# Adaptive-LN attention block on one core: the rounding of the weights' pieces from ScalarE to GpSimd, one transpose half a cycle later, and three portions of work moved behind empty ones

## The chip, the core and the metric

The kernel runs on one core of a Trainium2 chip. The metric is the device time of one execution in microseconds (us). A profiled execution also has a span, from its first to its last instruction; its own time is a little longer than that.

## What is computed

The input x is 2048 tokens by 512 features, in float32. Six rows of 512 come from silu(c) times a weight matrix; they scale, shift and gate the two halves of a transformer block:

```python
h = _layernorm(x, axis=-1) * (1 + ca) + sa
x = x + ga * _A_ref(h, A_wq, A_wk, A_wv, A_wo)
h = _layernorm(x, axis=-1) * (1 + cb) + sb
x = x + gb * _B_ref(h, B_w1, B_w2)
```

_A_ref is attention with 32 query heads of width 16 that share one key and one value head; scores are scaled, softmaxed over all 2048 keys, multiplied into the values and projected by wo. _B_ref is two dense layers, 512 to 1792 to 512, with a ReLU between them.

## The kernel before, in words

**Precision.** Many matmuls take their operands as float32r, a rounded float32. To keep accuracy, an operand is split in two pieces: a high piece, which is the value rounded to float32r, and a low piece, the rest. The product then takes three matmuls (high by high, high by low, low by high; `thrice`, L470). The helper `split` (L239) makes the pieces: ScalarE rounds with a Copy activation (L240) and GpSimd subtracts (L241). It serves weights, queries, the attention's output (`oh`, `ol`), the second layer norm's output (`hh`, `hl`), the hidden layer (`r4`) and the row maxima (`ms`).

**The main loop.** Attention is done in 32 units: 8 blocks of 256 tokens by 4 groups of 8 heads. A unit has 16 key tiles of 128. The loop at L884 runs 256 cycles, two key tiles each, so a unit lasts 8 cycles. A cycle has two parts, and the order of TensorE's work in each is written out by hand in `PARTS` (L40), one letter per step:

```python
PARTS = "cbcuaucuaucuau", "bldlbldlbldlad"
```

"c" and "d" are score matmuls, each into one of three PSUM banks `ps_exp`, which ScalarE reads with an Exp (L768, L770). "a" and "b" are the score matmuls of a later unit, into three banks `ps_max`, whose row maxima VectorE takes (L426, L428). "u" and "l" are the upper and lower 64 rows of a portion of other matmuls, the filling, all into the single bank `ps_fill` (L163). Each part ends with `values` (L872, L878), eight recorded matmuls into `ps_pv`; in the timeline one such group stands at the end of each part. The stretch between two such groups is called a half below, and cycles are counted from c = 0.

**Where other work hangs.** `advance` (L864) is the last piece of the sixth "l", that is near the end of part 2 of a cycle: it asks the generator of the filling for the next portion, and whatever the generator does between two portions is put into the engines' queues there. Work in the list `put_off` is issued in the next cycle's first part, after its fourth step (L913). Work in `half_later` is issued in the second part, after its second step (L916). At the end of a cycle the steps in `ends` that are due are issued (L920), and then one step of `chores` (L923). Each engine, and SP, which issues the DMAs, takes its instructions strictly in the order in which they were issued.

**Chores.** In c = 0 to 34 `chores` (L719) prepares the weights, one generator begun per cycle: 14 column blocks of w1 (`first_layer`: load, split, store the pieces to DRAM `w1dr`), 4 row blocks of wo (`projection`: load, multiply by the gate on GpSimd, split into `woh` and `wol`) and 14 row blocks of w2 (`second_layer`, the same into `w2r`). From c = 2 to 33 one split falls at the end of each cycle. The raw blocks rotate through three buffers.

**Filling.** In c = 0 to 32 the filling is the projection of queries 3 to 13 (`others_of`, L708), three portions each, of float32 matmuls; after the third, `end` (L341) copies the bank to `stg` on ScalarE (L248) and puts off the split into `qq` and the three stores to DRAM (`to_dram`, L337). From c = 33 on, each block b = 0 to 6 has 32 cycles of filling by `behind(b)` (L511), one portion per cycle: three portions `rest`, four of the output projection, seven of `fill`, fourteen of the first dense layer, four of the second. For b > 0, `fill` is the second dense layer of the block before. For the first of them, b = 0, `rest` is query 14, and `fill` is query 15 (three portions) and four empty ones (L527); an empty portion is replaced by six matmuls whose result nobody reads (L898). The two `qq` tiles of b = 0 share three buffers `w1s` with the tiles that first-layer weights are loaded into (`load_w1`, L450).

**The second layer norm.** While `fill` runs, `second_norm` (L557) goes one step further at each `advance`. Its steps: put off `norm_of(0)`, which normalises the first tile of 128 tokens (a few small VectorE and GpSimd instructions, then three large ones on GpSimd); statistics of the second tile on VectorE; `norm_of(1)` and `turn_of(0)`; `turn_of(1)` by way of `half_later`; two cycles on, four loads of `xh` from DRAM `xdr`; and put off the split of `xh` into `hh` and `hl`, which the first dense layer needs in the cycle after. `turn_of` (L542) transposes a tile in 32 by 32 blocks on VectorE (`xt`, L544) and stores it to `xdr` (L546, on SP's queue). In this kernel block b = 0 does these steps in c = 39 to 45; block b = 1 does them 32 cycles later, and so on.

**The end of a unit.** `normalise` (L773) copies `ps_pv` to `pvs` on ScalarE (L780) at the end of a unit's last cycle, c = 7, 15, 23 and so on. Two cycles later `back` (L803) takes reciprocals (L804) and issues `recs` (L805) and `den` (L806) on SP; `den` must wait for `recs` to land.

The last block is finished by `behind_last` after the loop; it doesn't touch the changed lines.

Of the kernel before, what the change touches and what calls it, by code (L numbers as in the profile page):

```python
# [9 lines left out]
F32 = mybir.dt.float32  # L10
# [3 lines left out]
OP = mybir.AluOpType  # L14
# [42 lines left out]
def build(tc, nc, cst, sb, ps, dr, x, wq, wk, wv, wo, w1, w2, c, w_mod, out):  # L57
# [8 lines left out]
    def ps_fill():  # L66
        return ps.tile([P, 512], F32, name="ps_fill", tag="fill", bufs=1)
# [51 lines left out]
    woh = cst.tile([P, DC, D], F32R, name="woh")  # L119
    wol = cst.tile([P, DC, D], F32R, name="wol")  # L120
# [118 lines left out]
    def split(hi, lo, src, eng=None):  # L239
        nc.scalar.activation(hi, src, AF.Copy)  # L240
        (eng or nc.gpsimd).tensor_tensor(lo, src, hi.bitcast(F32), op=OP.subtract)  # L241

    def stage():
        return sb.tile([P, 512], F32, name="stg", tag="stg", bufs=3)
# [11 lines left out]
    put_off, half_later = [], []  # L256

    def add_psum(dst, pt, other):
        stg = stage()
        nc.scalar.activation(stg, pt, AF.Copy)  # L260
        nc.gpsimd.tensor_tensor(dst, stg, other, op=OP.add)  # L261
# [185 lines left out]
    w2r = []  # L447
# [13 lines left out]
    def flat(t, k2):  # L461
        return t[:, k2 * 2:k2 * 2 + 2].rearrange("p a n -> p (a n)")

    def open_block(b):
        x1 = sb.tile([P, TT, D], F32, name="x1", tag="x1", bufs=2)
        nc.sync.dma_start(x1, chunks(x[b * TB:(b + 1) * TB]))
        x1s[b] = x1
        return x1, [sb.tile([P, DC, TB], F32R, name=n, tag="t4", bufs=2) for n in ("oh", "ol")]
# [23 lines left out]
    def dense2(b, t, pt):  # L492
        ts = slice(t * P, (t + 1) * P)
        todo = []
        for f in range(FC):
            i, fi = divmod(f, 8)
            rh, rl = r4s[b][i * 2], r4s[b][i * 2 + 1]
            w = w2r[f // 2]
            for n, (a, p) in enumerate(((rh, 0), (rh, 1), (rl, 0))):
                todo.append(("f32r", pt, a[:, fi, ts], w[:, p, f % 2],  # L500
                             f + n == 0, f == FC - 1 and n == 2))
        return todo
# [8 lines left out]
    def behind(b):  # L511
        def in_parts(todo, n):
            for i in range(0, len(todo), n):
                yield todo[i:i + n]

        def second(b, t):
            pt = ps_fill()
            yield from in_parts(dense2(b, t, pt), 6)
            ot = sb.tile([P, D], F32, name="ot", tag="tmp", bufs=2)
            add_psum(ot, pt, x1s[b][:, t])  # L520
            nc.sync.dma_start(out[b * TB + t * P:b * TB + (t + 1) * P], ot)

        x1, oo = open_block(b)
        if b == 0:
            qqs = [sb.tile([P, 2, LB], F32R, name="qq", tag="w1s", bufs=3) for _ in range(2)]
            rest, fill = [others_of(14 + n, qqs[n]) for n in range(2)]
            fill = itertools.chain(fill, [[]] * 4)  # L527
        else:
            rest, fill = carried.pop(), second(b - 1, 1)
        yield next(rest)  # L530
        yield next(rest)
        for k2 in range(DC // 2):
            put_off.append(partial(split, flat(oo[0], k2), flat(oo[1], k2), flat(on[b], k2)))
        yield from rest
        xn = sb.tile([P, TT, D], F32, name="xn", tag="xn", bufs=1)
        xdr = dr.tile([32, TT, 4, D], F32, name="xdr", tag="xdr", bufs=2)
        mvs = [ln_mv(1) for t in range(TT)]

        def norm_of(t):
            normed(x1, xn, (t,), *ln_stats(mvs[t], 1, False), nc.gpsimd)  # L540

        def turn_of(t):  # L542
            xt = sb.tile([P, D], F32, name="xt", tag="tmp", bufs=2)
            nc.vector.transpose(xt.rearrange("p (j k n) -> p k j n", j=4, k=DC),  # L544
                                xn[:, t].rearrange("p (k j n) -> p k j n", j=4, k=DC))
            nc.sync.dma_start(xdr[:, t].rearrange("a i n -> i a n"), xt)  # L546

        for t in range(TT):
            pt = ps_fill()
            for n, part in enumerate(in_parts(out_proj(pt, oo, t), 6)):  # L550
                yield part
                if t and n == 0:
                    ln_sums(mvs[0], 0, x1[:, 0])
            add_psum(x1[:, t], pt, x1[:, t])
        ahead = [load_w1(f) for f in range(2)]

        def second_norm():  # L557
            put_off.append(partial(norm_of, 0))
            yield
            ln_sums(mvs[1], 0, x1[:, 1])  # L560
            yield
            norm_of(1)
            turn_of(0)
            yield
            half_later.append(partial(turn_of, 1))
            yield
            yield
            xh = sb.tile([P, TT * 4, DC, 32], F32, name="xh", tag="xn", bufs=1)
            pieces = xdr.rearrange("a t i (j m) -> j a (t i) m", j=4)
            for j in range(4):  # L570
                nc.sync.dma_start(xh[j * 32:(j + 1) * 32].rearrange("p q k n -> p q (k n)"),
                                  pieces[j])
            yield
            for k2 in range(DC // 2):
                ks = slice(k2 * 2, k2 * 2 + 2)
                put_off.append(partial(split, *[h[:, ks].rearrange("p k (q n) -> p k q n", n=32)
                                                for h in hp],
                                       xh.rearrange("p q k n -> p k q n")[:, ks]))
            yield

        norm2 = second_norm()
        next(norm2)
        hp = [sb.tile([P, DC, TB], F32R, name=n, tag="t4", bufs=2) for n in ("hh", "hl")]
        for n, part in enumerate(fill):
            yield part
            next(norm2, None)
        r4 = r4s[b] = [sb.tile([P, 8, TB], F32R, name="r4", tag="big", bufs=4) for _ in range(4)]
        for f2 in range(FC // 2):
            pt = ps_fill()
            for f in range(f2 * 2, f2 * 2 + 2):  # L590
                if f + 2 < FC:
                    ahead.append(load_w1(f + 2))
                yield dense1(pt[:, (f % 2) * TB:(f % 2 + 1) * TB], ahead.pop(0), hp)
            i, f = divmod(f2 * 2, 8)
            put_off.append(split_psum(
                r4[i * 2][:, f:f + 2].rearrange("p a n -> p (a n)"),
                r4[i * 2 + 1][:, f:f + 2].rearrange("p a n -> p (a n)"), pt, AF.Relu))
        first_half = second(b, 0)
        yield from itertools.islice(first_half, 4)
        carried.append(first_half)  # L600
# [118 lines left out]
    def chores():  # L719


        def first_layer(f):
            raw = sb.tile([P, DC, P], F32, name="raw", tag="stg", bufs=3)
            nc.sync.dma_start(raw, chunks(w1[:, f * P:(f + 1) * P]))
            yield
            yield
            parts = sb.tile([P, 2, DC, P], F32R, name="w1s", tag="w1s", bufs=3)
            split(parts[:, 0], parts[:, 1], raw)
            yield
            nc.sync.dma_start(w1dr[f].bitcast(F32), parts.bitcast(F32))  # L730
            yield

        def projection(i):
            raw = sb.tile([P, D], F32, name="raw", tag="stg", bufs=3)
            nc.sync.dma_start(raw, wo[i * P:(i + 1) * P])
            yield
            nc.gpsimd.tensor_tensor(raw, raw, gr[:, 0], op=OP.mult)
            yield
            split(woh[:, i], wol[:, i], raw)
            yield  # L740
            yield

        def second_layer(f):
            raw = sb.tile([P, D], F32, name="raw", tag="stg", bufs=3)
            nc.sync.dma_start(raw, w2[f * P:(f + 1) * P])
            yield
            nc.gpsimd.tensor_tensor(raw, raw, gr[:, 1], op=OP.mult)
            yield
            if f % 2 == 0:
                w2r.append(sb.tile([P, 2, 2, D], F32R, name="w2r", tag="wt", bufs=7))  # L750
            split(w2r[-1][:, 0, f % 2], w2r[-1][:, 1, f % 2], raw)
            yield
            yield

        todo = [first_layer(f) for f in range(FC)] + [projection(i) for i in range(DC)] \
            + [second_layer(f) for f in range(FC)]
        for n in range(len(todo) + 3):

            for g in todo[max(0, n - 3):n + 1]:
                next(g)  # L760
            yield
# [122 lines left out]
    for c in range(NU * KT // 2):  # L884
# [5 lines left out]
        if places:  # L890
            u, i, j = places.pop(0)
# [69 lines left out]
```

## Time and profile before

| | us |
|---|---|
| three executions: median | 1662.97 |
| lowest and highest of the three | 1656.94, 1666.34 |
| the profiled execution's own time | 1652.57 |
| its span | 1650.8 |
| PE, DVE, ACT, POOL busy in the span | 1631.9, 1359.6, 1220.1, 361.7 |

PE is TensorE's matmuls, PEld its weight loads, DVE is VectorE, ACT ScalarE, POOL GpSimd, and SPq the queue of SyncE, which issues DMAs. A row of the view of stretches gives a stretch of the span from A to B, its length, and the busy time of each engine in it with the number of instructions. A row of the timeline gives a start, a busy time, the engine, the line, the operation, what it writes and reads, and in brackets how long the engine was idle just before and whose end let it go on. Durations of instructions on one engine overlap a little, since the next one enters before the last one has drained.

### The profile page before, as it was taken

Reading aid. Unit: us, or ns where it says so; the run is one execution under the profiler, and the core shown is the slowest. Engines: PE = TensorE matmul, PEld = TensorE weight load, DVE = VectorE, ACT = ScalarE, POOL = GpSimd, SP = SyncE. Lnnn points to the kernel's source line nnn. Section 1 sums busy time; section 2 is a strip of 40 time slices with the busy share of each in tenths; the row PEclk is TensorE's granted clock in tenths of the full one; section 3 lists DMA queues with packets and bytes.
Section 4 is the critical chain, followed back from the end, with each engine's and each line's share of the span. In section 5 each row is a group of like instructions: output and inputs, shape, how many; then the busy total and the mean of one; then the engine's idle time right before and its main releaser. Section 6 shows DMA issues by size and latency. Waiting matters only on the chain.

```text
span 1650.8 us, 33967 instructions
## 1 busy us (share of the span) xinstructions
PE 1631.9 (99%) x13018; PEld 918.2 (56%) x13018; DVE 1359.6 (82%) x2371; ACT 1220.1 (74%) x2385; POOL 361.7 (22%) x524
## 2 busy tenths in 40 slices
PE   8999999999999999999999999999999999999999
PEld 5445555555655565546654565446654565556568
DVE  7888888898889988898889888898889888897031
ACT  4248888877877788778877787778877888778831
POOL 3103355331103211131103211131113211131110
PEclk9999999999999999999999999999999999999999
DMA  8115543223301231113301231113211231113331
GB/s 287 51 51 161 186 128 111 88 71 99 104 17 49 73 105 55 43 56 105 93 28 38 74 117 43 62 42 110 83 30 39 84 106 41 61 43 102 122 113 57
DMA packets 97544, 137.19 MB, mean 83 GB/s; under 512 B 25644, under 2 KB 60396, under 8 KB 97384
## 3 DMA queue, kind: packets, MB, share of 16 engines
q1 hardware_dynamic: 95672, 134.90, 26.5%
q8 instruction: 104, 1.70, 0.4%
q14 instruction: 56, 0.46, 0.1%
q10 hardware_dynamic: 1712, 0.13, 0.1%
HBM read 104.00 MB, written 28.82 MB: 80 GB/s over the span
## 4 chain that ended last, share of the span: by engine, by line
PE 90%; ACT 4%; DVE 2%; DMA 1%; issue 1%; SPq 0%; POOL 0%; POOLq 0%; ACTq 0%; DVEq 0%
PE ps_pv L878 29%; PE ps_exp L768 21%; PE ps_max L426 18%; PE ps_fill L163 16%; ACT pe L770 3%; PE ps_exp L146 2%; PE ps_max L146 1%; DVE pm L428 1%; PE ps_fill L146 1%; PE ps_exp L307 1%; PE ps_exp L190 1%; DMA wmod<-in_w_mod_dram 0%; DMA xdr<-xt 0%; PE ps_exp L293 0%; PE ps_fill L190 0%
## 5 line engine op out<-in xcount | busy, mean ns | idle before, releaser
L428 DVE TENSOR_REDUCE pm<-ps_max 128x1 f32<-128x512 f32 x2048 | 1272.5, 682 | 166.2 <-PE ps_max L426 140.9
L770 ACT ACTIVATE pe<-ps_exp 128x512 f32<-128x512 f32 x2048 | 1080.7, 606 | 290.7 <-PE ps_fill L163 134.3
L426 PE MATMUL ps_max<-kp,qp 48*128 48x512 f32 x2048 | 846.4, 426 | 1.1 <-DVE pm L428 0.3
L768 PE MATMUL ps_exp<-qp,kp 50*128 50x512 f32 x2048 | 763.4, 414 | 5.0 <-ACT pe L770 3.3
L878 PE MATMUL ps_pv<-pe,vt 128*32 128x512 f32 x4096 | 545.5, 605 | 0.0
L426 PEld LDWEIGHTS ps_max<-kp,qp 48*128 48x128 f32 x2048 | 372.5, 185 | 274.6 <-DVE pm L428 240.4
L768 PEld LDWEIGHTS ps_exp<-qp,kp 50*128 50x128 f32 x2048 | 360.2, 185 | 267.0 <-ACT pe L770 180.2
L163 PE MATMUL ps_fill<-w2r,r 64*128 64x512 f32 x1044 | 288.8, 405 | 0.0
L163 PE MATMUL ps_fill<-hh,w1s 64*128 64x256 f32 x1568 | 229.0, 285 | 0.0
L163 PEld LDWEIGHTS ps_fill<-hh,w1s 64*128 64x128 f32 x1568 | 204.5, 186 | 6.7 <-PEq L156 6.7
L163 PEld LDWEIGHTS ps_fill<-w2r,r 64*128 64x128 f32 x1044 | 181.9, 185 | 7.1 <-PEq L156 2.5
L878 PEld LDWEIGHTS ps_pv<-pe,vt 128*32 128x32 f32 x4096 | 80.5, 108 | 125.9 <-issue 105.7
L241 POOL TENSOR_TENSOR r<-stg,r 128x512 fp32r<-128x512 f32 x49 | 62.7, 1280 | 320.6 <-ACT r L240 303.7
L163 PE MATMUL ps_fill<-hl,w1s 64*128 64x256 f32 x784 | 126.8, 281 | 0.0
L163 PE MATMUL ps_fill<-hT,wq 64*128 64x256 f32 x416 | 118.2, 399 | 0.0
L163 PEld LDWEIGHTS ps_fill<-hl,w1s 64*128 64x128 f32 x784 | 105.8, 186 | 0.0
L922 POOL TENSOR_TENSOR on<-num,den 128x256 f32<-128x256 f32 x31 | 22.8, 737 | 244.9 <-DMA den<-recs 204.9
L163 PEld LDWEIGHTS ps_fill<-hT,wq 64*128 64x128 f32 x416 | 70.2, 185 | 2.9
L784 POOL COPY num<-pvs 128x256 f32<-128x256 f32 x32 | 12.7, 397 | 173.5 <-ACT pvs L780 173.5
L261 POOL TENSOR_TENSOR x<-stg,x 128x512 f32<-128x512 f32 x14 | 18.2, 1297 | 97.9 <-ACT stg L260 97.9
L633 DVE TENSOR_TENSOR ol<-on,oh 128x256 fp32r<-128x256 f32 (+1 forms) x3 | 2.1, 714 | 44.2 <-ACT oh L629 44.2
L248 ACT ACTIVATE stg<-ps_fill 128x512 f32<-128x512 f32 x62 | 38.3, 617 | 0.0
(145 smaller groups left out, 931.0 us busy)
## 6 DMA issues: line engine op xcount, KB each, us to landing
w1s<-w1dr SPq DMA_DIRECT2D x104, 512.0 KB
qdr<-qq SPq DMA_DIRECT2D x48, 256.0 KB
qp<-qdr SPq DMA_DIRECT2D x128, 96.0 KB
raw<-in_B_w_dram SPq DMA_DIRECT2D x28, 256.0 KB
w1dr<-w1s SPq DMA_DIRECT2D x14, 512.0 KB
wmod<-in_w_mod_dram SPq DMA_DIRECT2D x6, 1024.0 KB
x<-in_A_x_dram SPq DMA_DIRECT2D x8, 512.0 KB
out_dram<-ot SPq DMA_DIRECT2D x16, 256.0 KB
```

The costliest lines, as they stand in the source:

```text
L146: nc.tensor.matmul(pt, w, a, start=start, stop=stop)
L163: ins = nc.tensor.matmul(pt, w[r], a[r], start=start and h == 1, stop=stop and h == 0)
L190: nc.tensor.matmul(pt, sgw[:, k], wm[i][:, k], start=k == 0, stop=k == DC - 1)
L241: (eng or nc.gpsimd).tensor_tensor(lo, src, hi.bitcast(F32), op=OP.subtract)
L248: nc.scalar.activation(stg, pt, func, **kw)
L261: nc.gpsimd.tensor_tensor(dst, stg, other, op=OP.add)
L426: nc.tensor.matmul(pt, qps[u][i][r, j * P:(j + 1) * P], kp[r, kb * 512:(kb + 1) * 512], start=True, stop=True)
L428: nc.vector.tensor_reduce(pms[u][:, (i * 2 + hf) * 4 + j, kb:kb + 1], pt, axis=AX.X, op=OP.max)
L768: nc.tensor.matmul(pt, kp[r, kt * P:(kt + 1) * P], qps[u][ct // 2][r], start=True, stop=True)
L770: nc.scalar.activation(pe, pt, AF.Exp)
L878: nc.tensor.matmul(pvt[i * 32:(i + 1) * 32], vt[:, kt], pes.pop((s, i)), start=(kt == 0), stop=(kt == KT - 1))
L922: due[1]()
```

## The change

- In the three chores `split` is replaced by a new helper, `split_pool`, which has GpSimd do the rounding as well as the subtraction. That is 14 + 4 + 14 = 32 roundings of a 128 x 512 block; all other splits stay.
- `turn_of(0)` isn't issued at `advance`, straight behind `norm_of(1)`, but put off: it comes in the first part of the next cycle, after its fourth step. It does so in all seven blocks.
- For b = 0, `fill` is three empty portions, the three of query 15 and one empty portion, in place of the three of query 15 and four empty ones.

```diff
+    def split_pool(hi, lo, src):
+        nc.gpsimd.tensor_copy(hi, src)
+        nc.gpsimd.tensor_tensor(lo, src, hi.bitcast(F32), op=OP.subtract)
...
-            fill = itertools.chain(fill, [[]] * 4)
+            fill = itertools.chain([[]] * 3, fill, [[]])
...
             norm_of(1)
-            turn_of(0)
+            put_off.append(partial(turn_of, 0))
             yield
             half_later.append(partial(turn_of, 1))
...
-            split(parts[:, 0], parts[:, 1], raw)
+            split_pool(parts[:, 0], parts[:, 1], raw)
...
-            split(woh[:, i], wol[:, i], raw)
+            split_pool(woh[:, i], wol[:, i], raw)
...
-            split(w2r[-1][:, 0, f % 2], w2r[-1][:, 1, f % 2], raw)
+            split_pool(w2r[-1][:, 0, f % 2], w2r[-1][:, 1, f % 2], raw)
```

## The prediction

> **What bounds the kernel now.** I read the page first, then lengths of stretches, then single halves. The page's span, engines and chain:
>
> ```profile
> span 1650.8 us, 33967 instructions
> PE 1631.9 (99%) x13018; PEld 918.2 (56%) x13018; DVE 1359.6 (82%) x2371; ACT 1220.1 (74%) x2385; POOL 361.7 (22%) x524
> PE 90%; ACT 4%; DVE 2%; DMA 1%; issue 1%; SPq 0%; POOL 0%; POOLq 0%; ACTq 0%; DVEq 0%
> ```
>
> TensorE is the bound; GpSimd is on the chain nowhere. The change takes no matmul away, so all that it can win is places where TensorE waits. They show in the lengths of stretches, cut where `ps_pv` groups start (view of stretches: length, then PE, PEld, DVE, ACT, POOL busy):
>
> ```profile
> 106.55:118.11 11.56, 11.56 (x89) 6.29 (x87) 9.84 (x17) 8.36 (x17) 0.00 (x0) 1.00 0.55 155
> 106.55:313.63 207.08, 204.29 (x1496) 107.56 (x1494) 176.09 (x293) 173.18 (x343) 82.88 (x73) 1.00 0.46 139
> 402.72:482.77 80.05, 80.05 (x744) 47.87 (x742) 70.48 (x119) 65.02 (x129) 10.38 (x12) 1.00 0.23 69
> 280.82:284.01 3.19, 3.08 (x24) 1.37 (x23) 2.81 (x5) 3.19 (x8) 1.12 (x1) 1.00 0.04 8
> 316.46:319.31 2.85, 2.85 (x23) 1.34 (x22) 2.46 (x5) 2.80 (x7) 0.04 (x1) 1.00 0.00 0
> 197.85:201.30 3.45, 3.08 (x24) 1.37 (x23) 3.06 (x5) 3.30 (x8) 1.51 (x2) 1.00 0.52 191
> 388.32:391.30 2.98, 2.98 (x30) 1.88 (x28) 2.58 (x5) 2.78 (x7) 0.40 (x1) 1.00 0.57 176
> 537.55:540.94 3.39, 3.32 (x24) 1.33 (x23) 3.32 (x9) 2.85 (x7) 1.64 (x9) 1.00 0.07 8
> 546.63:549.46 2.83, 2.83 (x24) 1.55 (x22) 2.51 (x6) 1.82 (x5) 0.70 (x1) 1.00 0.62 185
> 351.56:355.17 3.61, 3.52 (x22) 1.45 (x21) 3.54 (x10) 3.07 (x7) 1.79 (x10) 1.00 0.07 10
> 377.94:382.62 4.68, 3.36 (x24) 1.42 (x22) 3.13 (x7) 3.08 (x7) 2.38 (x2) 1.00 0.17 46
> ```
>
> The third row is 14 quiet cycles, 5.72 us each, so a half is about 2.85 and there TensorE is never idle. The first is c = 0 and 1, before any weight is split: 5.78 a cycle, since float32 query portions cost a little more. The second is all 35 cycles of the chores. At 5.78 they would take 202.3; they take 207.1. **So the chores' stage holds 4.8 us of waiting, and no more can be won there.** The other rows are single halves: the undisturbed kind is 2.85, the rest are what the change goes for.
>
> **Part 1: rounding on GpSimd.** The half from 280.82 takes 3.19 us with ScalarE busy all through. Its ScalarE timeline, and the weight load that waited:
>
> ```profile
> 281.20 0.62 ACT L248 ACTIVATE stg<-ps_fill 128x512 f32<-128x512 f32 x1
> 281.67 0.63 ACT L770 ACTIVATE pe<-ps_exp 128x512 f32<-128x512 f32 x1
> 282.15 0.66 ACT L240 ACTIVATE w2r<-raw 128x512 fp32r<-128x512 f32 x1
> 282.67 1.12 ACT L770 ACTIVATE pe<-ps_exp 128x512 f32<-128x512 f32 x2
> 283.62 0.68 ACT L240 ACTIVATE qq<-stg 128x512 fp32r<-128x512 f32 x1
> ```
> ```profile
> 283.35 0.18 PEld L768 LDWEIGHTS ps_exp<-qp,kp 50*128 50x128 f32 x1 [0.54 <-ACT pe L770]
> ```
>
> Queries' copy `stg`, an exp, the weight's rounding, and only then the exp that frees the bank TensorE wants. The half from 316.46 is the control: the same copy and rounding of queries, no weight; it takes 2.85. In a chores' half the float32 portion adds 0.09 (5.78 against 5.69). So a rounding that meets `stg` costs 3.19 - 2.94 = 0.25. A query ends at c = 2, 5, ..., 32, eleven times, ten of them apart from a unit's end: **2.5 us**. The half from 197.85 is the other kind: `pvs` and a rounding behind it, 3.45; from 388.32, `pvs` alone, 2.98, or 3.07 with float32 portions. That is 0.38, at c = 7, 15 and 31, and some 0.5 at c = 23 where all three meet: **1.6**. A rounding in any other cycle costs nothing even now. Sum **4.1**; bounds 2.5 (the second kind not won) and 4.8 (all waiting there).
>
> What is added on GpSimd: 32 copies of 128 x 512. No such copy is in the trace; the nearest row is half as wide:
>
> ```profile
> L784 POOL COPY num<-pvs 128x256 f32<-128x256 f32 x4 | 1.6, 396 | 13.7 <-ACT pvs L780 13.7
> ```
> ```profile
> L241 POOL TENSOR_TENSOR w1s<-raw,w1s 128x512 fp32r<-128x512 f32 x14 | 18.0, 1284 | 72.6 <-ACT w1s L240 63.0 <-DMA qp<-mdr 4.8 <-DMA qdr<-qq 2.8
> ```
>
> Twice 396 is 0.79 us; the two-input row, 1.28, is the upper bound, 0.40 the lower. I take 0.79, the same operation: 25 us more on a GpSimd that is busy 82.9 of these 207.1, so 52%. What hides it is that idle time, and most of it goes: the second row shows GpSimd waiting 63 us for ScalarE's rounding of w1 alone. That wait vanishes, since both steps then follow each other on one queue, and what is late next is the raw block's DMA. Behind the copies on GpSimd queue the gate's product, the subtractions of `qq` and `ms`, `num` and `on`; SP waits for some of them (`w1dr`, `qdr`, `mdr`, and a raw block needs its buffer free). All are due cycles later, so 0.79 more or less is nothing to TensorE: cost 0. Without that cover it would be the whole 25 us.
>
> **Part 2: the first turning.** VectorE's timeline in the half from 537.55 (c = 73 into 74), and the load that waited:
>
> ```profile
> 538.40 0.15 DVE L222 TENSOR_SCALAR y<-y 128x1 int32<-128x1 int32 x1
> 538.48 0.70 DVE L544 STREAM_TRANSPOSE xt<-xn 128x512 f32<-128x512 f32 x1
> 539.10 0.65 DVE L428 TENSOR_REDUCE pm<-ps_max 128x1 f32<-128x512 f32 x1
> 539.67 0.23 DVE L804 RECIPROCAL rc<-rc 128x16 f32<-128x16 f32 x1
> ```
> ```profile
> 539.81 0.18 PEld L426 LDWEIGHTS ps_max<-kp,qp 48*128 48x128 f32 x1 [0.50 <-DVE pm L428]
> ```
>
> Small instructions, the transpose and a reciprocal come together; the maxima start late and the half takes 3.39, that is 0.54 too long. The second tile's transpose, issued after the second step of a part, costs nothing:
>
> ```profile
> 548.77 0.70 DVE L544 STREAM_TRANSPOSE xt<-xn 128x512 f32<-128x512 f32 x1
> ```
>
> It lies in the half from 546.63, 2.83 long. After the change the small instructions and the reciprocal stay at the boundary, and the transpose comes two maxima later. The first maximum behind the small instructions then starts where the transpose stood, and lets its bank go near 539.2 (538.55 + 0.65), in place of 539.75; the transpose delays later maxima by some 0.6 and leaves perhaps 0.1. I take 0.44 won per block, **3.1** in seven; bounds 0.1 (the bursts still add up) and 0.54 each, so 0.7 and 3.8.
>
> The turning issues a DMA too. SP's queue in the same block:
>
> ```profile
> 539.20 0.60 SPq L546 DMA_DIRECT2D xdr<-xt  x1
> 539.93 0.40 SPq L805 DMA_DIRECT2D recs<-rc  x1
> 545.33 0.66 SPq L806 DMA_DIRECT2D den<-recs  x1
> 546.04 1.86 SPq L376 DMA_DIRECT2D qp<-qdr  x4
> 549.50 0.56 SPq L546 DMA_DIRECT2D xdr<-xt  x1
> 555.48 2.54 SPq L571 DMA_DIRECT2D xh<-xdr  x4
> ```
>
> The first `xdr` falls behind `recs` and `den`, whose wait for `recs` now holds it, to 546.0 at the worst. The second `xdr` still goes at 549.5, and `xh` needs both: the second is the late one, so cost 0.
>
> **Part 3: query 15 later.** In b = 0 the half from 377.94 takes 4.68, 1.83 too long:
>
> ```profile
> 379.54 1.15 ACT L240 ACTIVATE hh<-xh 128x512 fp32r<-128x512 f32 x2 [1.82 <-DMA xh<-xdr]
> ```
> ```profile
> 361.94 3.21 SPq L339 DMA_DIRECT2D qdr<-qq  x3
> 365.26 0.51 SPq L546 DMA_DIRECT2D xdr<-xt  x1
> 373.25 4.07 SPq L571 DMA_DIRECT2D xh<-xdr  x4
> ```
>
> ScalarE stands waiting for `xh`, and the exps behind it. The second `xdr` is issued behind query 15's three stores and takes 7.99 us until `xh` can be issued; in b = 1, without them, 549.50 to 555.48, 5.98. With the stores gone, it lands 2.0 sooner after its issue, and the issue itself comes up to 3.3 earlier (the stores held SP from 361.94 on), against 1.82 of waiting: **1.8 won**. Against it, query 15 now ends at c = 45, so `stg`, two `hh` and `qq` fall into one half on ScalarE: four instructions, about 2.1 us of its time beside four exps. The control half holds two such at 2.80 busy of 2.85; half of the surplus goes to the next halves: **0.4 lost** (bounds 0 and 1.2). Its stores now stand ahead of the load of the third first-layer block, which reuses `qq`'s buffer but is needed two cycles later: 0. The float32 portions move, none is added; but in the half from 351.56 one lay on top of the turning (3.61 against 3.39): **0.2 won**.
>
> **Sum.** 4.1 + 3.1 + 1.8 - 0.4 + 0.2 = 8.8 us. The profiled execution's own 1652.57 becomes 1643.8. The runs' median, 1662.97, stands 10.4 above it, with nothing in the profile to say why; I carry the 8.8 over: **1654.2**.
>
> **The rivals.**
> *The turning only moves its wait* (0.1 per block): the bursts are under a microsecond apart. The free second transpose speaks against it. 8.8 - 2.4 = 6.4 won, 1656.6.
> *ScalarE stays the bound where it is loaded*: only 2.5 won in the chores and 1.2 lost at c = 46, thus 6.4, also 1656.6. For it: the control half is already 98% busy.
> *It doesn't do what it says*: `xh` is late for another reason, and part 3 gives -0.2 in place of +1.6: 7.0 won, 1656.0. The 5.98 of b = 1 speaks against it.
> *Slower: GpSimd's copies hold up VectorE*, if both engines' ways to SBUF collide. Place: the chores; price: at most the copies' 25 us on the path of the maxima, so 1663.0 - 4.7 + 25 = 1683; it decides once copies delay maxima by more than the 0.7 that the free second transpose delayed them by. The maxima in the chores and in the quiet stretch:
>
> ```profile
> L428 DVE TENSOR_REDUCE pm<-ps_max 128x1 f32<-128x512 f32 x281 | 174.8, 683 | 30.5 <-PE ps_max L426 26.1 <-PE ps_exp L768 4.1
> ```
> ```profile
> L428 DVE TENSOR_REDUCE pm<-ps_max 128x1 f32<-128x512 f32 x114 | 70.8, 683 | 9.3 <-PE ps_max L426 7.8 <-PE ps_exp L768 0.8 <-PE ps_fill L163 0.6
> ```
>
> 683 ns in both, with GpSimd busy 40% and 13%: against it. The Trainium skill's "GPSIMD Engine Reference", section 1 (Specifications), says that GpSimd's SBUF interfaces are shared with VectorE, with contention for VectorE instructions in a 2-port mode or with two SBUF inputs. The maxima read one PSUM input, so by that page they wouldn't be held up, and the trace agrees, 683 against 683; for a copy in place of a subtraction no run here shows it yet.
>
> **How the numbers follow.** Forecast, 7.8 to 10 won: 0.52. Turning only moved: 0.18. ScalarE stays the bound: 0.12. Part 3 not won: 0.08. Two of these at once, or `xh` late in all blocks, 4 won to 4 lost: 0.06. Slower: 0.04. A measurement of this kernel tells about 0.5%, 8.3 us, from no change, and the forecast lies just beyond: faster 0.49 (forecast 0.45, others 0.04), same 0.46, slower 0.05. Most that the bounds allow is 4.8 + 3.8 + 1.8 + 0.2 = 10.6, 1652.4, and the runs shown lie up to 6.0 below their median: low 1646. Least in 9 of 10 is about 3 won, 1660, and the runs lie up to 3.4 above: high 1663.
>
> **What would show it.** Right, step by step: halves at c = 2, 5, ... of 2.94 and no weight's rounding on ScalarE; the 35 cycles near 203 us; copies on GpSimd near 0.79 and maxima still 683; the half with the first turning under 3.0; no `xh` wait at c = 46 and that half near 3.2. Wrong: a waiting maximum behind the moved transpose, `xh` waits in later blocks, longer maxima, or TensorE waiting for `qp` behind SP.

## The result, and the profile after

| | before | changed |
|---|---|---|
| median of 22 executions each, us | 1659.61 | 1650.43 |
| ratio, with its 95% interval | | 0.9947 (0.9930 to 0.9964) |
| span of the profiled execution, us | 1650.8 | 1648.9 |
| main loop in it (first `ps_pv` group of c = 0 to that of c = 255), us | 1472.23 | 1463.59 |

The change makes the kernel 0.53% faster, 8.8 us by the ratio. One of the changed kernel's 22 executions took 3724.31 us, for a reason that nothing here shows, and the ratio leaves it out. The two profiled spans differ by only 1.9, and this is the first thing to read rightly: a span also holds the lead-in ahead of the loop. Two rows of the view of stretches, before and then changed, with TensorE's granted clock as the third figure from the end:

```profile
0.00:106.55 106.55, 99.11 (x387) 51.00 (x387) 86.85 (x198) 35.09 (x57) 20.96 (x35) 0.94 0.41 134
```
```profile
0.00:113.36 113.36, 103.79 (x387) 53.47 (x387) 89.37 (x198) 35.09 (x57) 21.07 (x35) 0.89 0.39 126
```

The changed kernel's lead-in has the same instructions, but TensorE was granted 0.89 of its clock there and not 0.94, and it took 6.8 us longer. In other runs below the loop begins anywhere from 110.7 to 120.6. So the comparisons below are made on the loop, where the clock is 1.00 and halves repeat to a few hundredths. Its rows, before and then changed:

```profile
106.55:1578.78 1472.23, 1466.85 (x12262) 812.68 (x12261) 1252.73 (x2135) 1175.59 (x2313) 335.01 (x483) 1.00 0.26 79
```
```profile
113.36:1576.95 1463.59, 1462.69 (x12262) 814.12 (x12261) 1251.78 (x2135) 1160.06 (x2281) 353.57 (x515) 1.00 0.26 79
```

The loop is 8.64 us shorter, which agrees with the timed 8.8.

The page of the changed kernel:

```profile
span 1648.9 us, 33974 instructions
PE 1632.5 (99%) x13018; PEld 922.2 (56%) x13018; DVE 1361.1 (83%) x2371; ACT 1204.5 (73%) x2353; POOL 380.4 (23%) x556
PE 94%; ACT 2%; DVE 2%; POOL 1%; issue 1%; DMA 0%; POOLq 0%; ACTq 0%; SPq 0%; DVEq 0%
```

ScalarE has 32 instructions fewer and GpSimd 32 more; ScalarE's share of the chain fell from 4% to 2%. The stretches that answer to those of before:

```profile
113.36:316.04 202.68, 202.60 (x1496) 108.99 (x1495) 175.75 (x293) 157.96 (x311) 101.02 (x104) 1.00 0.46 141
...
403.84:483.85 80.01, 80.01 (x744) 47.94 (x742) 70.50 (x119) 65.04 (x129) 10.37 (x12) 1.00 0.23 69
284.20:287.15 2.95, 2.95 (x24) 1.50 (x23) 2.55 (x5) 2.89 (x7) 0.38 (x1) 1.00 0.20 46
202.94:205.88 2.94, 2.94 (x23) 1.40 (x22) 2.55 (x5) 2.79 (x7) 1.06 (x3) 1.00 0.52 194
316.04:319.51 3.47, 3.35 (x21) 1.59 (x20) 3.02 (x5) 2.76 (x7) 3.21 (x3) 1.00 0.13 37
380.49:383.75 3.26, 3.26 (x25) 1.42 (x23) 2.92 (x5) 3.26 (x8) 2.90 (x3) 1.00 0.13 18
354.39:357.24 2.85, 2.85 (x25) 1.41 (x23) 2.78 (x8) 2.31 (x6) 1.25 (x7) 1.00 0.04 6
538.60:541.45 2.85, 2.85 (x25) 1.40 (x23) 2.78 (x8) 2.31 (x6) 1.26 (x7) 1.00 0.03 3
541.45:544.38 2.93, 2.93 (x24) 1.33 (x22) 2.93 (x6) 1.90 (x5) 2.33 (x8) 1.00 0.19 53
```

In order: the 35 cycles of the chores take 202.68 in place of 207.08, 4.40 won, and TensorE is busy for all but 0.08 of them. The 14 quiet cycles are what they were (80.05). A half where a query ends is now 2.95 (3.19 before), one behind a unit's end 2.94 (3.45). Then a half that nothing foretold: the second part of c = 35, 2.83 before, takes 3.47. The half with `xh` at c = 46 takes 3.26 (4.68), the first turning's half in b = 0 2.85 (3.61) and in b = 1 2.85 (3.39), and the one behind it 2.93 (2.84).

GpSimd's two instructions of a piece, and VectorE's maxima, over the same 35 cycles (groups: busy time, mean ns, idle time before and what ended it):

```profile
L244 POOL CAST w1s<-raw 128x512 fp32r<-128x512 f32 x14 | 8.6, 615 | 32.4 <-DMA raw<-in_B_w_dram 32.4
...
L245 POOL TENSOR_TENSOR w1s<-raw,w1s 128x512 fp32r<-128x512 f32 x14 | 18.0, 1284 | 1.1
...
L432 DVE TENSOR_REDUCE pm<-ps_max 128x1 f32<-128x512 f32 x281 | 174.5, 683 | 26.4 <-PE ps_max L430 22.5 <-PE ps_exp L772 3.9
```

A rounding takes 0.615 us on GpSimd. The subtraction's wait, 72.6 us of which 63.0 for ScalarE, is down to 1.1; what GpSimd waits for now is the raw block. The maxima still take 683 ns.

VectorE in b = 1, c = 73 into 74:

```profile
539.53 0.68 DVE L432 TENSOR_REDUCE pm<-ps_max 128x1 f32<-128x512 f32 x1
540.13 0.24 DVE L808 RECIPROCAL rc<-rc 128x16 f32<-128x16 f32 x1
540.28 0.63 DVE L432 TENSOR_REDUCE pm<-ps_max 128x1 f32<-128x512 f32 x1
540.83 0.70 DVE L548 STREAM_TRANSPOSE xt<-xn 128x512 f32<-128x512 f32 x1
```

The transpose stands two maxima later than it did. Its half lost all of its 0.54; the next gained 0.09.

### The profile page after: what moved, and what is told of

It reads as the page before. It is cut to its first block, busy times and chain, and to the rows that moved or that the text cites. A ratio compares the mean times of both kernels' runs of the same rounds, so it can differ in the third digit from the quotient of the medians.

```text
span 1648.9 us, 33974 instructions
## 1 busy us (share of the span) xinstructions
PE 1632.5 (99%) x13018; PEld 922.2 (56%) x13018; DVE 1361.1 (83%) x2371; ACT 1204.5 (73%) x2353; POOL 380.4 (23%) x556
## 4 chain that ended last, share of the span: by engine, by line
PE 94%; ACT 2%; DVE 2%; POOL 1%; issue 1%; DMA 0%; POOLq 0%; ACTq 0%; SPq 0%; DVEq 0%
PE ps_pv L882 30%; PE ps_exp L772 21%; PE ps_max L430 18%; PE ps_fill L163 18%; PE ps_exp L146 2%; ACT pe L774 1%; PE ps_max L146 1%; PE ps_exp L311 1%; PE ps_fill L146 1%; PE ps_fill L137 1%; PE ps_exp L297 1%; PE ps_exp L190 1%; PE ps_fill L190 0%; DVE st L208 0%; ACT pvs L784 0%
## 5 line engine op out<-in xcount | busy, mean ns | idle before, releaser
L241 POOL TENSOR_TENSOR ms<-sq,ms 128x32 fp32r<-128x32 f32 x32 | 8.1, 252 | 147.0 <-ACT ms L240 147.0
```

## The experiments

The first theory is that of the prediction: each part takes away waits of its own. The rivals: the waits move, depend on each other, or have another cause. Losses and gains are of the loop, against before's 1472.23, unless the text says otherwise.

### Each part alone

Only the pieces (`split_pool` in the three chores, nothing else):

```diff
-            split(parts[:, 0], parts[:, 1], raw)
+            split_pool(parts[:, 0], parts[:, 1], raw)
```

> The kernel before with only the weights' pieces rounded on GpSimd. Theory (each part removes its own waits, independently of the others): from the first ps_pv group to cycle 35 the loop is 4.4 us shorter than before, the half after c = 35 shows a new wait of about 0.6 (the output projection's second rounding waits for the last normalised product), the halves with the first turning stay at 3.39 and c = 46 stays near 4.7; in all 3.8 us less, a ratio near 0.998. Rival (the part's gain in the full change came with the other two, or the copies hold up VectorE): less than 2 us, or maxima above 683 ns in the chores.

Measured: ratio 0.9991 (0.9972 to 1.0010), which tells nothing from no change by itself. Its trace does:

```profile
118.69:1587.58 1468.89, 1465.84 (x12262) 815.04 (x12261) 1252.54 (x2135) 1160.46 (x2281) 353.76 (x515) 1.00 0.26 79
118.69:321.38 202.69, 202.60 (x1497) 109.08 (x1495) 175.73 (x293) 157.97 (x311) 100.89 (x104) 1.00 0.46 141
321.38:325.15 3.77, 3.35 (x21) 1.58 (x21) 3.03 (x5) 2.76 (x7) 3.21 (x3) 1.00 0.13 32
```

To c = 35 it wins the same 4.39, and the new wait behind it is there as well, 3.77. So both belong to this part. In all 3.34 are won where 3.8 were expected: the wait is 0.94 here, and 0.64 in the changed kernel, although both run the same instructions up to there. What sets its length is worked out below.

Only the turning:

```diff
-            turn_of(0)
+            put_off.append(partial(turn_of, 0))
```

> The kernel before with only the first tile's turning put off by half a cycle. Theory: in each of seven blocks the half with the turning goes from 3.39 to 2.85 and the next one from 2.84 to 2.94, 0.44 won each, 3.1 us in all, ratio near 0.998; cycle 35 and c = 46 as before. Rival (the wait only moves): the two halves together stay at 6.2 and nothing is won.

Measured: ratio 0.9989 (0.9970 to 1.0008); 3.74 won in the loop. In b = 1 to 6 it did what was expected (2.84 and 2.94 in b = 1). In b = 0 it did not. First the stretches of the half that leads from c = 43 into c = 44 and of the `xh` half at c = 46, then VectorE and SP there:

```profile
372.75:376.81 4.06, 3.71 (x24) 1.41 (x22) 3.56 (x6) 3.02 (x7) 0.00 (x0) 1.00 0.50 185
388.18:391.02 2.84, 2.84 (x24) 1.53 (x22) 2.52 (x6) 2.84 (x7) 2.42 (x2) 1.00 0.04 9
```
```profile
373.25 0.71 DVE L544 STREAM_TRANSPOSE xt<-xn 128x512 f32<-128x512 f32 x1 [1.12 <-DMA xdr<-xt]
```
```profile
365.33 0.66 SPq L806 DMA_DIRECT2D den<-recs  x1
366.08 0.59 SPq L546 DMA_DIRECT2D xdr<-xt  x1
```

The second transpose waited 1.12 us for the first tile's store, and the half is 1.2 too long; then the `xh` wait is gone. The two `xt` tiles share two buffers with query 15's `stg`. With the query between them, the second `xt` falls into the first one's buffer, and that one's store now stands behind `den` on SP. The part that moves the query takes it out from between. So the two parts are not independent, which no theory had said: without the third part, the second one has a price of 1.2 in b = 0. It is more than paid back there, since `xh` now lands in time and the half at c = 46 falls from 4.68 to 2.84. That is why this part alone wins 3.74 and not 3.1.

Only the order of the filling:

```diff
-            fill = itertools.chain(fill, [[]] * 4)
+            fill = itertools.chain([[]] * 3, fill, [[]])
```

> The kernel before with only query 15's portions behind three empty ones. Theory: the half at c = 46 goes from 4.69 to about 3.3 (the wait for xh is gone, four ScalarE instructions in one half leave 0.4), the halves where float32 portions lay on VectorE's bursts lose 0.2 each and three later ones gain 0.1 each: 1.5 us won, ratio near 0.999. Rival (xh is late for another reason): c = 46 stays above 4.5 and nothing is won.

Measured: ratio 1.0002 (0.9982 to 1.0022); the loop is 1.32 shorter (1.5 expected), and the half at c = 46 is 3.26 as in the full change:

```profile
384.48:387.74 3.26, 3.26 (x24) 1.43 (x23) 2.93 (x6) 3.26 (x8) 2.90 (x3) 1.00 0.13 19
```

The three parts alone win 3.34, 3.74 and 1.32, together 8.40; the full change wins 8.64. The nearness of the two is partly luck and doesn't show that the parts are independent: the wait for `xh` is won in the second run and again in the third, and the 1.2 is lost in the second alone.

### Is it the query's stores that made `xh` late?

The kernel before, the query in its place, but its stores issued later:

```diff
-            put_off.append(partial(to_dram, qt))
+            (stores_later if n_of(b, j) == 15 else put_off).append(partial(to_dram, qt))
...
+        while stores_later:
+            stores_later.pop(0)()
         r4 = r4s[b] = [...]
```

> The kernel before, query 15 where it was, but its three stores to DRAM issued five portions later, behind the loads of xh. Theory (the stores in front of the second xdr make xh late): the second xdr is issued about 1.4 us earlier, xh can be issued 6.0 us after it instead of 8.0, and the half at c = 46 falls from 4.69 to 2.9 or less, since no ScalarE instruction is added there. Rival (xh is late because of the queries' matmuls or ScalarE's or GpSimd's work for them, which stay): c = 46 stays above 4.5.

Measured in one execution: the half at c = 46, and SP's queue there:

```profile
388.39:391.24 2.85, 2.85 (x25) 1.55 (x23) 2.53 (x6) 2.85 (x7) 2.47 (x2) 1.00 0.34 77
```
```profile
374.19 0.57 SPq L549 DMA_DIRECT2D xdr<-xt  x1
380.10 2.55 SPq L574 DMA_DIRECT2D xh<-xdr  x4
```

4.68 fell to 2.85. From the second `xdr` to the first `xh` it is 5.91 us, as in other blocks, and 7.99 with the stores in front. The stores were the cause; neither the query's matmuls nor its ScalarE work was.

### Where does the wait behind c = 35 come from?

The changed kernel's queues there, ScalarE, then GpSimd:

```profile
315.60 0.63 ACT L240 ACTIVATE oh<-on 128x512 fp32r<-128x512 f32 x1
316.94 0.63 ACT L240 ACTIVATE oh<-on 128x512 fp32r<-128x512 f32 x1 [0.71 <-POOL on L926]
```
```profile
316.18 0.73 POOL L926 TENSOR_TENSOR on<-num,den 128x256 f32<-128x256 f32 x1 [5.87 <-DMA qp<-qdr]
```

ScalarE stands waiting for the last product `on`, and the exps behind it. Either GpSimd's copies hold something up, or the loop has outrun a chain of DMAs and of the work between them. Two kernels ask it, one with less and one with more of GpSimd's time. Less, a copy for the subtraction:

```diff
         nc.gpsimd.tensor_copy(hi, src)
-        nc.gpsimd.tensor_tensor(lo, src, hi.bitcast(F32), op=OP.subtract)
+        nc.gpsimd.tensor_copy(lo, src)
```

> The changed kernel with the subtraction of the weights' pieces replaced by a second copy, so that GpSimd has two copies of 0.64 per piece, the 1.28 that it had before the change (the low pieces then hold the weight itself, not the rest). It asks where the new wait after c = 35 (2.83 before, 3.47 after) comes from. Theory (the loop runs ahead of a chain of DMAs whose time is fixed, whatever GpSimd does): the half stays above 3.3. Rival (the copies delay GpSimd's queue and so SP's): it falls back to 2.85.

More:

```diff
         nc.gpsimd.tensor_copy(hi, src)
+        nc.gpsimd.tensor_copy(hi, src)
         nc.gpsimd.tensor_tensor(lo, src, hi.bitcast(F32), op=OP.subtract)
```

> The changed kernel with every one of the 32 roundings on GpSimd done twice, which is 20 us more of GpSimd's time in the chores (0.64 each). Theory (GpSimd's idle time hides the copies, and they don't hold up VectorE): the loop from the first ps_pv group to cycle 35 changes by less than 1 us, the maxima stay at 683 ns. Rival (the copies contend with VectorE or hold up what SP waits for): some us longer, up to 20, new waits in the chores, maxima above 683.

Measured, the half behind c = 35 in the first and in the second, then the second's 35 cycles:

```profile
314.23:317.46 3.23, 3.23 (x21) 1.58 (x20) 2.81 (x5) 2.76 (x7) 3.15 (x3) 1.00 0.15 43
```
```profile
319.46:322.57 3.11, 3.11 (x22) 1.59 (x21) 2.69 (x5) 2.76 (x7) 2.99 (x3) 1.00 0.12 38
```
```profile
116.76:319.46 202.70, 202.61 (x1497) 108.97 (x1495) 175.60 (x293) 157.97 (x311) 120.75 (x137) 1.00 0.46 141
```

With the subtraction's time back to what it was, the half is 3.23, under the 3.3 of the theory but far from the rival's 2.85; with 20 us of copies more it is 3.11, less than in the changed kernel. So it doesn't follow GpSimd's time. It follows a chain that starts with the copy of `ps_pv` at the unit's end. That copy's row and the product's, before; then the copy's row, changed:

```profile
293.75 0.60 ACT L780 ACTIVATE pvs<-ps_pv 128x512 f32<-128x512 f32 x1
```
```profile
312.84 0.73 POOL L922 TENSOR_TENSOR on<-num,den 128x256 f32<-128x256 f32 x1 [5.06 <-DMA qp<-qdr]
```
```profile
296.90 0.60 ACT L784 ACTIVATE pvs<-ps_pv 128x512 f32<-128x512 f32 x1
```

Before, the last product starts 19.09 us after the copy, and the half starts 19.88 after it (at 313.63). Changed, it is 19.28 (316.18) and 19.14 (316.04). The chain takes 19 us either way; the loop now gets there 0.74 sooner. Before, the product ended at 313.57 and the second rounding, which reads it, started at 313.7: the margin was about 0.1 on ScalarE. The chain is 0.19 longer now and the loop 0.74 sooner, 0.93 together, and the half grew by 0.64; so TensorE had some 0.3 to spare, and 0.64 of what the chores won is given back.

The same count in the other runs settles it. From the copy to the half it is 19.14 to 19.16 us in the four kernels below; from the copy to the product it differs, and the half differs with it:

| | copy to product, us | half behind c = 35, us |
|---|---|---|
| `copies_twice` | 18.92 | 3.11 |
| `same_pool_load` | 19.05 | 3.23 |
| changed | 19.28 | 3.47 |
| `pieces_alone` | 19.60 | 3.77 |

The half is the chain's time less 15.8 in all four. The spread lies mainly in its last step: from the issue of `den` to the product it is 3.16, 3.20, 3.48 and 3.82. Why that DMA takes longer in one execution than in another is not shown. GpSimd has a step in the chain too: `recs` stands on SP behind the stores of a query, whose subtraction starts 10.25 us after the copy before and 10.12 to 10.28 after it in these four, so the added copies don't delay it. The second execution confirms the rest: twice the copies cost the chores nothing (202.70 against 202.68).

How far does GpSimd's cover reach? Each rounding five times:

```diff
-        nc.gpsimd.tensor_copy(hi, src)
+        for _ in range(5):
+            nc.gpsimd.tensor_copy(hi, src)
```

> The changed kernel with every rounding on GpSimd done five times: 82 us more of GpSimd's time in the chores, some 185 of the 203 us of cycles 0 to 34. Theory (idle time hides the copies until GpSimd's queue is nearly full; then what SP waits for comes late): here the cover is nearly gone and waits of several us appear in or just behind the chores, with the maxima still at 683 ns. Rival (the copies are off the path whatever they take): the loop to cycle 35 changes by less than 1 us. Rival (contention with VectorE): maxima longer than 690 ns.

Measured: the 35 cycles, the half in the second part of c = 23, and the one behind c = 35; then the weight load that waited in the first of these halves, and ScalarE's wait in the second:

```profile
111.67:321.20 209.53, 206.13 (x1496) 110.30 (x1494) 175.99 (x293) 158.51 (x311) 174.80 (x227) 0.98 0.44 133
244.64:252.31 7.67, 4.27 (x22) 1.97 (x21) 3.24 (x6) 2.17 (x5) 7.06 (x11) 0.86 0.33 102
321.20:332.72 11.52, 4.04 (x22) 2.04 (x21) 3.09 (x5) 3.17 (x7) 6.99 (x9) 0.68 0.28 70
```
```profile
249.33 0.18 PEld L773 LDWEIGHTS ps_exp<-qp,kp 50*128 50x128 f32 x1 [3.51 <-DMA qp<-mdr]
```
```profile
329.49 0.63 ACT L240 ACTIVATE oh<-on 128x512 fp32r<-128x512 f32 x1 [8.09 <-POOL on L927]
```

With GpSimd busy 83% of the stretch, what is behind its copies comes too late at two places: the row maxima of the next unit (`ms`, then `mdr` and `qp`), and `on`. For `on`, the chain of above now takes 26.85 us: the query's subtraction, and so `recs`, comes 7 us later. The maxima on VectorE are still 682 ns. So contention is out, and the cover is real but ends between 120.75 and 174.80 us of GpSimd's time.

### Versions that go further

Two mends of the changed kernel: the attention output's second rounding goes into the second part of the cycle, and query 15 ends a cycle earlier.

```diff
-            fill = itertools.chain([[]] * 3, fill, [[]])
+            fill = itertools.chain([[]] * 2, fill, [[]] * 2)
...
-            put_off.append(partial(split, flat(oo[0], k2), flat(oo[1], k2), flat(on[b], k2)))
+            (half_later if k2 else put_off).append(
+                partial(split, flat(oo[0], k2), flat(oo[1], k2), flat(on[b], k2)))
```

> The changed kernel with the second half of each block's rounding of the attention output put into the second part of the cycle, and query 15 behind two empty portions with two after it. Theory: the wait after c = 35 goes from 3.47 to 2.9 or less, since the last product has half a cycle more; the half at c = 46 goes from 3.26 to 2.87, since the query's two ScalarE instructions now lie a cycle before the two of hh; in all 1 us less than the changed kernel's loop. Rival (ScalarE's load alone makes these halves long): the waits move to the next half and nothing is won.

Measured in one execution, the loop, the half behind c = 35, and that at c = 46:

```profile
110.67:1572.44 1461.77, 1460.99 (x12263) 812.94 (x12261) 1250.80 (x2135) 1160.43 (x2281) 354.42 (x515) 1.00 0.26 79
313.17:316.00 2.83, 2.83 (x21) 1.57 (x21) 2.41 (x5) 2.76 (x7) 2.76 (x3) 1.00 0.14 35
376.89:379.74 2.85, 2.85 (x24) 1.58 (x22) 2.51 (x6) 2.85 (x7) 2.49 (x2) 1.00 0.30 95
```

Both waits are gone; the loop is 1.82 shorter than the changed kernel's. The two halves make 1.05 of it; the rest is spread thinly over the loop, and one execution can't tell whether it belongs to the mends.

With these, VectorE's other bursts spread too: both statistics and the first turning behind the second step of the second part.

```diff
-                    ln_sums(mvs[0], 0, x1[:, 0])
+                    half_later.append(partial(ln_sums, mvs[0], 0, x1[:, 0]))
...
-            ln_sums(mvs[1], 0, x1[:, 1])
+            half_later.append(partial(ln_sums, mvs[1], 0, x1[:, 1]))
...
-            put_off.append(partial(turn_of, 0))
+            half_later.append(partial(turn_of, 0))
```

> The two mends, and besides the first turning another half cycle later and the second layer norm's two statistics put into the second part of a cycle, as the second turning is. Theory (a burst on VectorE of up to 0.7 us costs nothing behind the second step of a cycle's second part): in each of seven blocks the halves of 3.05 twice and 2.94 once fall to 2.85, 0.5 won each, 3.5 us in all; with the 1 us of the mends 4.5 less than the changed kernel, 13 less than before, ratio to before 0.992. Rival (0.87 of statistics is too long for that place, or xh comes late): the waits appear a half later and less than 1.5 us is won.

Measured: ratio to before 0.9950 (0.9929 to 0.9972), no better than the changed kernel; loop 1463.82. In b = 1 the halves with the statistics fell to 2.85 and 2.84, from 3.05 and 3.06 in the changed kernel, and the one behind the turning to 2.84, but the half with the small instructions went from 2.85 to 3.59. In it VectorE shows why, and the load that waits:

```profile
540.29 0.69 DVE L208 BATCH_NORM_STATS2 st<-x 128x6 f32<-128x512 f32 x1
...
542.29 0.14 DVE L220 TENSOR_SCALAR ve<-mv 128x1 f32<-128x1 f32 x1
```
```profile
543.46 0.18 PEld L430 LDWEIGHTS ps_max<-kp,qp 48*128 48x128 f32 x1 [0.69 <-DVE pm L432]
```

The second statistics now end just ahead of `norm_of(1)`'s small instructions, and the two bursts add up: the first rival of this run, and the one that the prediction named for the turning. So the second statistics go back:

```diff
-            half_later.append(partial(ln_sums, mvs[1], 0, x1[:, 1]))
+            ln_sums(mvs[1], 0, x1[:, 1])
```

> The two mends, the first tile's statistics behind the second step of a cycle's second part, and the first turning another half cycle later; the second tile's statistics stay where the changed kernel has them. Theory (a burst on VectorE is free there if no other burst follows within half a cycle; the second statistics were followed by the small instructions of norm_of(1), which is why that half took 3.60): per block one half falls from 3.05 to 2.85 and one from 2.94 to 2.85, the half with the small instructions stays at 2.85; 0.3 per block, 2 us less than with the two mends, 12.5 less than before in the loop, ratio to before about 0.9925. Rival (VectorE's load of the whole stretch decides, wherever the bursts lie): the half after the moved turning or the one with the small instructions grows by as much as is won.

Measured: ratio to before 0.9933 (0.9910 to 0.9956), loop 1459.89, that is 12.34 won against 8.64, near the 12.5 expected. In b = 1:

```profile
526.54:529.39 2.85, 2.85 (x24) 1.35 (x22) 2.47 (x5) 2.32 (x6) 0.00 (x0) 1.00 0.03 10
538.25:541.30 3.05, 3.05 (x24) 1.37 (x22) 3.02 (x6) 2.51 (x7) 2.70 (x5) 1.00 0.07 13
544.14:547.00 2.86, 2.86 (x25) 1.40 (x23) 2.79 (x9) 2.32 (x6) 1.27 (x7) 1.00 0.03 3
547.00:549.83 2.83, 2.83 (x25) 1.56 (x23) 2.55 (x6) 1.82 (x5) 2.23 (x8) 1.00 0.14 46
```

The first statistics' half, the second's (unmoved, 3.05), the small instructions' and the turning's: no half pays for another here. By the loop this is the best version; by time its interval overlaps the changed kernel's.

## Why the prediction was right, step by step

- **The sum**, 8.8 us: 8.64 in the loop and 8.8 by the ratio. The mechanisms of the three parts were right. Two terms came out worse, the cost of 0 by 0.64 and the 0.2 of the float32 portions, of which nothing came. Part 1 and the turning won 0.3 and 0.2 more than forecast, and some 0.2 came in differences of a few hundredths all over the loop. That these nearly make up for each other is luck.
- **Part 1, 4.1 won**: 4.40. A query's end was worth 0.24 (0.25 worked out); a unit's end 0.51 and not 0.38, because the copy `pvs` alone costs nothing on top of a float32 portion: 2.94, not 3.07. At c = 23, where all three meet, it was worth 0.51 as well (3.69 to 3.18; some 0.5 worked out).
- **Its cost of 0** failed. The step was that what is due from GpSimd and SP is due "cycles later". The copies were indeed hidden, at 0.615 us each where 0.79 was taken. But `on` was due with a margin of about 0.1 on ScalarE and some 0.3 on TensorE, at the end of a chain that doesn't get shorter with the loop: 0.64 lost.
- **Part 2, 0.44 a block**: in b = 1 to 6 0.54 to 0.57 won and 0.08 to 0.10 lost, 0.47 on average. The cost of 0 on SP held for b = 1 to 6. For b = 0 it held only with part 3; alone the turning pays 1.2, for the buffer that the working had left out. The wait that was to hold the first `xdr`, 5.40 from `recs` to `den` in b = 1, got shorter with `xdr` out of its way: 1.42 there in the changed kernel, and 2.3 in b = 0 of the turning alone, against 5.29 before.
- **Part 3, 1.8 won and 0.4 lost**: 4.68 to 3.26, that is 1.42, and 0.41 left above 2.85. `stores_late` shows the cause of the wait to be the one named. The loss came out as forecast, but not from four ScalarE instructions in one half: `stg` runs a half earlier (378.00), and the exps wait for three roundings in a row, two of `hh` and `qq` (380.13 to 381.81). Two of `hh` alone cost nothing (2.85 in `stores_late`), and with the query a cycle earlier the loss is gone.
- **Its 0.2 from the float32 portions** was mis-sized: the working counted one of the two halves that they left and none that they went to. Where they left they gave 0.4, where they went they cost 0.4 (halves of 2.94, 3.06 and 2.94 in place of 2.84, 2.86 and 2.85), so nothing.
- **The time**, 1654.2 against 1650.43: the 8.8 were set on the median of three executions, 1662.97; over 22 it is 1659.61, and that is 3.4 of the 3.8 between them.

Of the rivals, the turning that only moves its wait didn't come true here, but did in another place, in the run with everything spread. ScalarE didn't stay the bound: the chores won 4.40 and not 2.5, and c = 46 lost 0.41 and not 1.2. The contention of GpSimd with VectorE didn't occur even with five copies for one. The Trainium skill's "GPSIMD Engine Reference", section 1 (Specifications), which the prediction cited, names contention only for VectorE instructions in a 2-port mode or with two SBUF inputs. The trace agrees, 682 ns with five copies and 683 without any, and these runs show it for copies too.

## What to carry to other kernels

In a loop whose bound engine is always busy, cut the trace at a repeated landmark, list the stretches that are longer than their kind, and find for each a sister stretch that lacks one instruction: the difference is a price. The halves that changed by more than 0.04 us account for 8.45 of the loop's 8.64. Whatever speeds up the loop also uses up the margin of chains whose time is fixed, here one with several DMAs, so the nearest of these belongs in the sum with its margin. In these runs a burst of 0.70 or 0.87 us on VectorE behind the second step of a part was free where no other burst followed within half a cycle, and cost 0.74 where one did; and a moved instruction moves its tile in the rotation of buffers too.

## What the runs showed of the hardware that was not expected

- The lead-in's granted clock differs from execution to execution (0.94, 0.89 and, in the last version, 0.83), and the loop's start with it (106.55, 113.36 and 120.60). These 14 us are more than the whole change; the loop's lengths repeat far better.
- TensorE's granted clock fell with its long waits: in the run with five copies, the halves where its weight loads waited 3.51 and 7.93 us show 0.86 and 0.68 of the clock, where the same halves of the changed kernel show 1.00.
- Rounding float32 to float32r on GpSimd takes 0.615 us for 128 x 512, where a ScalarE rounding took 0.65 and a two-input subtraction on GpSimd takes 1.28.
